# Split f32r products in place of fp32 ones for the first weight of a fused attention and expert kernel

## The chip, the cores and the metric

The kernel runs on one core of a Trainium2 chip, in one launch. The metric is the device time of one execution in microseconds (us). The engines are TensorE (PE, with its weight loads shown apart as PEld), VectorE (DVE), ScalarE (ACT), GpSimd (POOL) and SyncE (SP), which here issues most of the DMAs. Each engine works its own list of instructions in order, and waits on semaphores for the others.

## The reference

Attention over a small set of packed queries, then two feed-forward blocks:

```python
p_packed = softmax(scale * p @ k.T) @ v           # 4 batches, 8 heads, 32 rows of 64
out      = softmax(scale * q @ p_packed.T) @ p_packed
x = out.transpose(0, 2, 1, 3).reshape(2304, 512)  # 4 batches of 576 tokens, 8 heads * 64
h = x @ w_in                                      # 512 -> 2048
x = (max(h, 0) + log1p(exp(-abs(h)))) @ w_out     # softplus, 2048 -> 512
out = (sigmoid(x @ w_gate) * (x @ w_val)) @ w_out2
```

The weights of the two blocks arrive as 64-bit floats; the kernel reads them as pairs of 32-bit words and builds 32-bit floats from them.

## The kernel before

**Stages.** The first stage is attention, worked in eight units of half a batch (`attn_unit`). The second is the softplus block, which overlaps the end of the first. Its hidden width of 2048 is cut into eight chunks `c` of 256 columns. The third is the gated block. The change touches the second stage, and one small operation in the first.

**How x @ w_in is worked.** x of a batch is the second softmax (A2, kept as an f32r pair `A2h`, `A2l`) times the packed rows pp. So the kernel forms pp @ w_in first, for each chunk, and multiplies A2 by that. pp lies in `bdT`, block by block. Chunks 0 and 1 are formed batch by batch (`prep_wp_one`), chunk 2 for two batches at once (`prep_wp_two`), and chunks 3 to 7 for all four (`prep_wp_four`, since `FOUR = 3`). For the last, POOL copies each unit's pp into `ppq` (L472), in an order in which one matmul of 64 rows serves four batches: 128 columns of the array are four batches of 32 rows. Two such matmuls, of the upper and the lower 64 partitions, go to two PSUM banks. They are plain fp32 (L645). ACT copies each bank into a `cv` tile (L652), sixteen DMAs on SP sort its parts by batch into two `xs` tiles (L656), and POOL splits those into f32r pairs `wph` and `wpl` (`split_wp`, `hi_of` and `split_lo`, helper lines L104 and L101).

**The split.** An f32r matmul takes operands cut to fewer bits. To keep the accuracy, an operand is written as hi + lo, and a product as three f32r matmuls: hi*hi, hi*lo, lo*hi (`mm3`, L113 to L115). All large products of the kernel are made so.

**The loop around it.** For a batch b, a chunk c and a half s of its tokens, `emit_h` issues twelve f32r matmuls of 288 columns into a two-bank PSUM tile, ACT forms softplus (L697), ACT and POOL split it into `ghl` (L108, L101), and two turns later `emit_out1` multiplies it by `w_out`: four banks of six matmuls (L725, L726, L728), each added by DVE into `xa` (L733). `ghl` must be complete for the last two of the six.

**What sets the order.** The weights are prepared by generators in a queue `jobs`: `tick()` runs the next step of the first one, and is called four times in each `emit_out1`. `finish(name)` runs all steps that a job still lacks, at the place where its result is used. So a job with more steps ends later in the program, or is forced at `finish`. `prep_win` (conversion of w_in, DVE L180, L185, L189) and `prep_wo` (conversion and split of w_out) of a chunk are queued after the `wp` job of the chunk before. A conversion asks for the next raw weight when it ends, and there are two raw buffers (`NRAW = 2`). The instructions are then ordered on each engine by the framework's scheduler, so that the order on an engine is not that of the program text.

**Buffers.** The `cv` tiles are five, the one-bank PSUM tiles four, the `w_in` tiles two, the two-bank PSUM tiles two.

Of the kernel before, what the change touches and what calls it, by code (L numbers as in the profile page):

```python
# [9 lines left out]
F32 = mybir.dt.float32  # L10
F32R = mybir.dt.float32r
# [3 lines left out]
ALU = mybir.AluOpType  # L15
# [6 lines left out]
def attn_moe_moe_kernel(  # L22
# [21 lines left out]
    nc = tc.nc  # L44
    B, H, S, D = q.shape
    NK = p.shape[2]
# [3 lines left out]
    P = 128  # L50
    NC = 6
    CT = S // NC
    HS = S // 2
# [46 lines left out]
    def split_lo(eng, lo, x, hi):  # L100
        eng.tensor_tensor(lo, x, hi.bitcast(F32), op=ALU.subtract)  # L101

    def pool_hi(hi, x):
        nc.gpsimd.tensor_scalar(hi, x, 1.0, 0.0, op0=ALU.mult, op1=ALU.add)  # L104

    def hi_of(on_act, hi, x):
        if on_act:
            nc.scalar.activation(hi, x, AF.Copy)  # L108
        else:
            pool_hi(hi, x)  # L110
# [54 lines left out]
    def convert(key, dst):  # L165

        t = raws.pop(key)
        hw, lw = t[:, :, 1], t[:, :, 0]  # L170
        if len(dst.shape) == 3:
            hw = hw.rearrange("p (k n) -> p k n", k=KD)
            lw = lw.rearrange("p (k n) -> p k n", k=KD)
        to = x = dst.bitcast(I32)
        if cps[0] and dst.space != PSUM:
            x = bank1()
            if len(dst.shape) == 3:
                x = x.rearrange("p (k n) -> p k n", k=KD)
            x = x.bitcast(I32)
        nc.vector.tensor_scalar(  # L180
            x, hw, 3, 0x3FFFFFF8, op0=ALU.logical_shift_left, op1=ALU.bitwise_and
        )
        if not cps[0]:
            yield
        nc.vector.scalar_tensor_tensor(  # L185
            x, hw, -0x40000000, x, op0=ALU.bitwise_and, op1=ALU.bitwise_or
        )
        yield
        nc.vector.scalar_tensor_tensor(  # L189
            to, lw, 29, x, op0=ALU.logical_shift_right, op1=ALU.bitwise_or  # L190
        )
        load_next()
# [84 lines left out]

    bdT = ph1.tile([P, 2 * B + 2, P], F32, name="bdT")

    ppq = ph1.tile([P, 2 * KD // 2, B, NK], F32, name="ppq")  # L280

    pT = [att.tile([P, 4 * P], F32, name=f"pT{i}") for i in range(2)]
    for t in pT:
# [61 lines left out]
    def heads(tile_, start, step):  # L345

        return tile_[:, start : start + 2 * step].rearrange("p (j x) -> p j x", x=step)[
            :, :, :NK
        ]
# [33 lines left out]
    def attn_unit(u):  # L383
# [81 lines left out]
        for e in range(2):  # L465
            r = slice(64 * e, 64 * e + 64)
            to = bdT[r].rearrange("p j n -> p (j n)")
            copy(
                BDA, heads(to, 512 * half + 256 * g + 64 * odd + 32 * e, 64 if odd else 192),
                heads(pp[r], 32 * e, 64),  # L470
            )
            nc.gpsimd.tensor_scalar(  # L472
                ppq[r, 2 * g : 2 * g + 2, b],
                heads(to, 512 * half + 256 * g + 64 * odd + 32 * e, 64 if odd else 192),
                1.0, 0.0, op0=ALU.mult, op1=ALU.add,
            )
        yield
        a2s = []
        for hf in range(2):
# [84 lines left out]
        return xa[:, i : i + KD * HS].rearrange("p (m t) -> p m t", m=KD)  # L564

    def prep_win(c):
        wt = ph1.tile([P, KD, CF], F32, tag="w_in", bufs=2, name="w_in")
        for f in range(2):
            yield from convert(("in", c, f), wt[:, :, f * P : (f + 1) * P])
            yield  # L570
        w_in_f[c] = wt
# [60 lines left out]

    xs = {}

    def prep_wp_four(c):

        wt = w_in_f[c]
        for half in range(2):
            xs[half, c] = ph1.tile([P, 2, 2, CF], F32, tag="xs", bufs=3, name="xs")
        for j in range(2):  # L640
            ps = [bank1().rearrange("p (t n) -> p t n", t=2) for _ in range(2)]
            for t in range(2):
                for e in range(2):
                    r = slice(64 * e, 64 * e + 64)
                    nc.tensor.matmul(  # L645
                        ps[e][:, t, :], ppq[r, 2 * t + j].rearrange("p b n -> p (b n)"),
                        wt[r, 2 * t + j, :], start=True, stop=True,
                    )
            yield
            for e in range(2):  # L650
                x = new_cv().rearrange("p (t n) -> p t n", t=2)
                nc.scalar.activation(x, ps[e], AF.Copy)  # L652
                for b in range(B):
                    half, odd = divmod(b, 2)
                    o = 64 * (odd ^ j) + 32 * e
                    nc.sync.dma_start(xs[half, c][o : o + 32, odd], x[32 * b : 32 * b + 32])  # L656
                yield

    def split_wp(half, c):
        for odd in range(2):  # L660
            hi, lo = wp_tiles()
            x = xs[half, c][:, odd]
            hi_of(WPH, hi, x)
            split_lo(nc.gpsimd, lo, x, hi)
            Wp[2 * half + odd, c] = (hi, lo)
            yield

    def prep_wp_half(half, c):
        if c < FOUR:
            yield from prep_wp_two(half, c)  # L670
            return
        if half == 0:
            yield from prep_wp_four(c)
        yield from split_wp(half, c)

# [157 lines left out]
    def new_cv():  # L833
        return cv.tile([P, DM], F32, tag="cv", name="cv")
# [323 lines left out]
```

## Time and profile before

| | us |
|---|---|
| median of 3 runs | 861.76 (861.45 to 863.3) |
| the profiled execution | 862.72 |
| span of its instructions | 860.6 |
| PE busy | 839.2 (98%) |
| DVE busy | 588.4 (68%) |
| POOL busy | 479.8 (56%) |
| ACT busy | 326.5 (38%) |

Some 2 us of the execution lie outside the span. Busy times overlap each other. A matmul's duration in the trace runs from its start until its last result is out, so neighbours overlap: the pace of a stream of matmuls is the distance between starts, not the duration. An fp32 matmul stands in the trace as two records.

### The profile page before, as it was taken

How to read it: one execution, taken by the hardware profiler on the slowest of the kernel's cores; microseconds unless marked ns; L12 is line 12 of the kernel's file. 1: busy time of each engine (PE TensorE's matmuls, PEld its weight loads, DVE VectorE, ACT ScalarE, POOL GpSimd, SP SyncE). 2: the span in 40 equal slices, each digit the busy share in tenths (PEclk: the TensorE clock that was granted, in tenths of full speed). 3: DMA queues.
4: the chain of work that ended last, by engine and by line, in shares of the span. 5: the costliest groups of instructions: out<-in, count | busy, mean ns of one | idle time of the engine just before them, and what ended most of it. 6: DMA issues, size and time to landing. Idle time of an engine off the chain costs nothing. (4 is left out here: it accounts for less than half of the span.)

```text
span 860.6 us, 15689 instructions
## 1 busy us (share of the span) xinstructions
PE 839.2 (98%) x6112; PEld 783.0 (91%) x6112; DVE 588.4 (68%) x1004; ACT 326.5 (38%) x606; POOL 479.8 (56%) x469
## 2 busy tenths in 40 slices
PE   7899999999999999999989999999999999999997
PEld 5788989899989999999989999999989999999996
DVE  2776556946656375458788688897896656767665
ACT  4467575563333333434323422232352432322210
POOL 4564333245647364594579786886983734536400
PEclk9999999999999999999999999999999999999999
DMA  9984320203363233500155464644525412213003
GB/s 236 222 206 103 84 59 26 74 25 108 114 178 101 73 98 82 167 5 1 37 171 156 151 177 149 191 129 136 159 55 154 122 41 84 68 43 111 13 1 110
DMA packets 61864, 90.79 MB, mean 105 GB/s; under 512 B 7648, under 2 KB 40544, under 8 KB 61792
## 3 DMA queue, kind: packets, MB, share of 16 engines
q1 hardware_dynamic: 60784, 88.56, 36.9%
q10 hardware_dynamic: 1008, 1.25, 0.4%
q8 instruction: 48, 0.79, 0.4%
q14 instruction: 24, 0.20, 0.1%
HBM read 65.67 MB, written 18.87 MB: 98 GB/s over the span
## 5 line engine op out<-in xcount | busy, mean ns | idle before, releaser
L113 PE MATMUL bank<-aop,BH 128*128 128x288 f32 x672 | 199.1, 296 | 5.0 <-DVE work L1026 2.1
L115 PE MATMUL bank<-aop,BL 128*128 128x288 f32 x672 | 198.6, 296 | 0.0
L114 PE MATMUL bank<-aop,BH 128*128 128x288 f32 x672 | 197.8, 294 | 0.2 <-DVE aop L101 0.2
L733 DVE TENSOR_TENSOR xa<-xa,ps 128x288 f32<-128x288 f32 x224 | 99.5, 450 | 100.3 <-PE ps L728 100.1
L101 POOL TENSOR_TENSOR ghl<-g,ghl 128x576 fp32r<-128x576 f32 x64 | 93.5, 1463 | 132.1 <-ACT ghl L108 113.1
L725 PE MATMUL ps<-ghl,woh 128*128 128x288 f32 x512 | 146.4, 301 | 2.0 <-ACT cv L652 1.3
L726 PE MATMUL ps<-ghl,wol 128*128 128x288 f32 x512 | 143.6, 295 | 0.0
L113 PEld LDWEIGHTS bank<-aop,BH 128*128 128x128 f32 x672 | 126.2, 188 | 10.8 <-issue 2.5
L114 PEld LDWEIGHTS bank<-aop,BH 128*128 128x128 f32 x672 | 126.4, 188 | 4.2 <-DVE aop L101 0.4
L115 PEld LDWEIGHTS bank<-aop,BL 128*128 128x128 f32 x672 | 126.6, 188 | 0.0
L101 POOL TENSOR_TENSOR BL<-cv,BH 128x512 fp32r<-128x512 f32 (+1 forms) x96 | 117.2, 1235 | 3.4 <-ACT BH L108 2.4
L728 PE MATMUL ps<-ghl,woh 128*128 128x288 f32 x512 | 109.1, 294 | 0.1
L725 PEld LDWEIGHTS ps<-ghl,woh 128*128 128x128 f32 x512 | 96.2, 188 | 5.6 <-ACT cv L652 1.6
L726 PEld LDWEIGHTS ps<-ghl,wol 128*128 128x128 f32 x512 | 96.3, 188 | 0.2
L1026 DVE TENSOR_TENSOR work<-work,bank 128x576 f32<-128x576 f32 (+1 forms) x100 | 70.8, 725 | 31.5 <-PE bank L115 31.3
L1074 PE MATMUL ps<-ol,gv 128*128 128x512 f32 x216 | 84.9, 393 | 0.0
L1073 PE MATMUL ps<-oh,gv 128*128 128x512 f32 x216 | 84.3, 390 | 0.5 <-ACT gv L1039 0.4
L1075 PE MATMUL ps<-oh,gv 128*128 128x512 f32 x216 | 84.7, 393 | 0.0
L728 PEld LDWEIGHTS ps<-ghl,woh 128*128 128x128 f32 x512 | 82.2, 188 | 0.5 <-POOL ghl L101 0.5
L1081 DVE TENSOR_TENSOR xa<-xa,ps 128x512 f32<-128x512 f32 x90 | 61.5, 683 | 28.5 <-PE ps L1075 28.0
L104 POOL TENSOR_SCALAR BH<-cv 128x512 fp32r<-128x512 f32 (+1 forms) x48 | 30.0, 634 | 88.1 <-PE bank L114 87.8
L113 PE MATMUL ps<-A2h,wph 128*128 128x288 f32 x256 | 77.3, 302 | 0.4 <-ACT wph L595 0.4
(137 smaller groups left out, 1613.7 us busy)
## 6 DMA issues: line engine op xcount, KB each, us to landing
cv<-B SPq DMA_DIRECT2D x52, 256.0 KB, 2.7
B<-cv SPq DMA_DIRECT2D x48, 256.0 KB, 4.1
raw_in<-in_moe_w_in_dram SPq DMA_DIRECT2D x16, 512.0 KB, 3.7
raw_out<-in_moe_w_out_dram SPq DMA_DIRECT2D x16, 512.0 KB, 3.5
raw_g<-in_moe_w_gate_dram SPq DMA_DIRECT2D x12, 512.0 KB, 4.1
raw_v<-in_moe_w_val_dram SPq DMA_DIRECT2D x12, 512.0 KB, 4.4
raw_o<-in_moe_w_out_dram SPq DMA_DIRECT2D x12, 512.0 KB, 4.1
xs<-cv SPq DMA_DIRECT2D x80, 64.0 KB, 2.0
```

Source lines behind the costliest of these rows:

```text
L101: eng.tensor_tensor(lo, x, hi.bitcast(F32), op=ALU.subtract)
L113: nc.tensor.matmul(ps, wh, xh, start=first, stop=False)
L114: nc.tensor.matmul(ps, wh, xl, start=False, stop=False)
L115: nc.tensor.matmul(ps, wl, xh, start=False, stop=last)
L725: nc.tensor.matmul(out_, wh[:, ms], gh[:, f], start=f == 0, stop=False)
L726: nc.tensor.matmul(out_, wl[:, ms], gh[:, f], start=False, stop=False)
L728: nc.tensor.matmul(out_, wo_hl[c, f][0][:, ms], gl[:, f], start=False, stop=f == 1)
L733: nc.vector.tensor_tensor(dst, dst, out_, op=ALU.add)
L1026: nc.vector.tensor_tensor(to, x, y, op=ALU.add)
L1073: nc.tensor.matmul(bank, gh[:, ts_], oh, start=f == 0, stop=False)
L1074: nc.tensor.matmul(bank, gh[:, ts_], ol, start=False, stop=False)
L1075: nc.tensor.matmul(bank, gl[:, ts_], oh, start=False, stop=f == 1)
```

## The change

pp @ w_in of chunks 3 to 7 becomes three f32r products of split operands in place of one fp32 product.

- `ppq` becomes a pair of f32r tiles. It is no longer filled unit by unit in `attn_unit`. A generator `prep_ppq` of eight steps fills it at the start of chunk 3's `wp` job: 16 roundings (`pool_hi`) and 16 subtractions, all on POOL, each of 64 partitions by 64 elements.
- `prep_win` of chunks 3 to 7 converts into a `cv` tile; ACT rounds it into `hi` (`hi_of`, `WHA = 1`) and POOL subtracts (`split_lo`). The pair takes both `w_in` buffers, so that one chunk is held at a time, not two.
- `prep_wp_four` issues 12 f32r matmuls of 64 rows by 256 columns for each `j`, in place of 4 fp32 ones: 120 in all in place of 40.
- An `xs` tile is cut into two halves; four of them are held, and for odd chunks the second pair of batches uses the tiles `t1`.

```diff
@@ -277,7 +277,7 @@
 
     bdT = ph1.tile([P, 2 * B + 2, P], F32, name="bdT")
 
-    ppq = ph1.tile([P, 2 * KD // 2, B, NK], F32, name="ppq")
+    ppq = [ph1.tile([P, KD, B, NK], F32R, name=f"ppq{y}") for y in "hl"]
 
     pT = [att.tile([P, 4 * P], F32, name=f"pT{i}") for i in range(2)]
     for t in pT:
@@ -469,11 +469,6 @@
                 BDA, heads(to, 512 * half + 256 * g + 64 * odd + 32 * e, 64 if odd else 192),
                 heads(pp[r], 32 * e, 64),
             )
-            nc.gpsimd.tensor_scalar(
-                ppq[r, 2 * g : 2 * g + 2, b],
-                heads(to, 512 * half + 256 * g + 64 * odd + 32 * e, 64 if odd else 192),
-                1.0, 0.0, op0=ALU.mult, op1=ALU.add,
-            )
         yield
         a2s = []
         for hf in range(2):
@@ -564,6 +559,17 @@
         return xa[:, i : i + KD * HS].rearrange("p (m t) -> p m t", m=KD)
 
     def prep_win(c):
+        if c >= FOUR:
+            hl = [ph1.tile([P, KD, CF], F32R, tag="w_in", bufs=2, name="w_in") for _ in "hl"]
+            for f in range(2):
+                x = new_cv().rearrange("p (k n) -> p k n", k=KD)
+                yield from convert(("in", c, f), x)
+                hi, lo = (y[:, :, f * P : (f + 1) * P] for y in hl)
+                hi_of(WHA, hi, x)
+                split_lo(nc.gpsimd, lo, x, hi)
+                yield
+            w_in_f[c] = hl
+            return
         wt = ph1.tile([P, KD, CF], F32, tag="w_in", bufs=2, name="w_in")
         for f in range(2):
             yield from convert(("in", c, f), wt[:, :, f * P : (f + 1) * P])
@@ -632,20 +638,46 @@
 
     xs = {}
 
+    def prep_ppq():
+
+        for b in range(B):
+            half, odd = divmod(b, 2)
+            for e in range(2):
+                r = slice(64 * e, 64 * e + 64)
+                for g in range(2):
+                    src = heads(
+                        bdT[r].rearrange("p j n -> p (j n)"),
+                        512 * half + 256 * g + 64 * odd + 32 * e, 64 if odd else 192,
+                    )
+                    hi, lo = (y[r, 2 * g : 2 * g + 2, b] for y in ppq)
+                    pool_hi(hi, src)
+                    split_lo(nc.gpsimd, lo, src, hi)
+                yield
+
+    def xs_tile(half, c):
+        if half and c % 2:
+            t = ph1.tile([P, 2, HS], F32, tag="t1", bufs=2, name="t1")
+            t = t.rearrange("p f t -> p (f t)")[:, : 2 * CF]
+        else:
+            t = ph1.tile([P, 2 * CF], F32, tag="xs", bufs=4, name="xs")
+        return t.rearrange("p (t n) -> p t n", t=2)
+
     def prep_wp_four(c):
 
         wt = w_in_f[c]
         for half in range(2):
-            xs[half, c] = ph1.tile([P, 2, 2, CF], F32, tag="xs", bufs=3, name="xs")
+            xs[half, c] = [xs_tile(half, c) for _ in range(2)]
         for j in range(2):
             ps = [bank1().rearrange("p (t n) -> p t n", t=2) for _ in range(2)]
             for t in range(2):
-                for e in range(2):
-                    r = slice(64 * e, 64 * e + 64)
-                    nc.tensor.matmul(
-                        ps[e][:, t, :], ppq[r, 2 * t + j].rearrange("p b n -> p (b n)"),
-                        wt[r, 2 * t + j, :], start=True, stop=True,
-                    )
+                J = 2 * t + j
+                for n, (x, y) in enumerate(((0, 0), (0, 1), (1, 0))):
+                    for e in range(2):
+                        r = slice(64 * e, 64 * e + 64)
+                        nc.tensor.matmul(
+                            ps[e][:, t, :], ppq[x][r, J].rearrange("p b n -> p (b n)"),
+                            wt[y][r, J, :], start=n == 0, stop=n == 2,
+                        )
             yield
             for e in range(2):
                 x = new_cv().rearrange("p (t n) -> p t n", t=2)
@@ -653,13 +685,13 @@
                 for b in range(B):
                     half, odd = divmod(b, 2)
                     o = 64 * (odd ^ j) + 32 * e
-                    nc.sync.dma_start(xs[half, c][o : o + 32, odd], x[32 * b : 32 * b + 32])
+                    nc.sync.dma_start(xs[half, c][odd][o : o + 32], x[32 * b : 32 * b + 32])
                 yield
 
     def split_wp(half, c):
         for odd in range(2):
             hi, lo = wp_tiles()
-            x = xs[half, c][:, odd]
+            x = xs[half, c][odd]
             hi_of(WPH, hi, x)
             split_lo(nc.gpsimd, lo, x, hi)
             Wp[2 * half + odd, c] = (hi, lo)
@@ -670,6 +702,8 @@
             yield from prep_wp_two(half, c)
             return
         if half == 0:
+            if c == FOUR:
+                yield from prep_ppq()
             yield from prep_wp_four(c)
         yield from split_wp(half, c)
```

**POOL, where chunk 3's products are split.** POOL's list before; `ghl` is a softplus result of chunk 2, `wph` and `wpl` are chunk 3's pair, one for each batch, `xs` their source:

```order
L101 TENSOR_TENSOR ghl_2812<-g32_2774,ghl_2812 128x576
L101 TENSOR_TENSOR ghl_2884<-g32_2848,ghl_2884 128x576
L104 TENSOR_SCALAR wph_2872<-xs_2753 128x512
L101 TENSOR_TENSOR wpl_2873<-xs_2753,wph_2872 128x512
L104 TENSOR_SCALAR wph_2887<-xs_2753 128x512
L101 TENSOR_TENSOR wpl_2888<-xs_2753,wph_2887 128x512
L104 TENSOR_SCALAR wph_2922<-xs_2754 128x512
L104 TENSOR_SCALAR wph_2934<-xs_2754 128x512
L101 TENSOR_TENSOR wpl_2923<-xs_2754,wph_2922 128x512
L101 TENSOR_TENSOR wpl_2935<-xs_2754,wph_2934 128x512
L101 TENSOR_TENSOR ghl_2946<-g32_2912,ghl_2946 128x576
```

The same place on POOL now, after the same two `ghl` of chunk 2; `w_in_2981` is the lo half of chunk 4's w_in, `wol_3069` and `wol_3111` are chunk 4's w_out:

```order
L101 TENSOR_TENSOR w_in_2981<-cv_2982,w_in_2980 128x4x128
L101 TENSOR_TENSOR w_in_2981<-cv_3010,w_in_2980 128x4x128
L101 TENSOR_TENSOR wol_3069<-cv_3050,woh_3068 128x512
L101 TENSOR_TENSOR wol_3111<-cv_3080,woh_3110 128x512
L104 TENSOR_SCALAR wph_2933<-xs_2877 128x512
L101 TENSOR_TENSOR wpl_2934<-xs_2877,wph_2933 128x512
L104 TENSOR_SCALAR wph_2937<-xs_2878 128x512
L101 TENSOR_TENSOR wpl_2938<-xs_2878,wph_2937 128x512
L104 TENSOR_SCALAR wph_2941<-t1_2879 128x512
L104 TENSOR_SCALAR wph_2968<-t1_2880 128x512
L101 TENSOR_TENSOR wpl_2942<-t1_2879,wph_2941 128x512
L101 TENSOR_TENSOR wpl_2969<-t1_2880,wph_2968 128x512
```

Four operations of chunk 4's weights now stand ahead of chunk 3's first `wph`; before they stood after all of chunk 3's. The row that follows these is `ghl_2994`, the first softplus result of chunk 3.

**SP, the DMAs that sort chunk 3's products.** Before, where a row with x2 is two DMAs; `raw_out_2709` and `raw_out_2739` are the two halves of chunk 4's w_out:

```order
L656 DMA xs_2753<-cv_2798 32x512 x2
L656 DMA xs_2754<-cv_2798 32x512 x2
L656 DMA xs_2753<-cv_2829 32x512 x2
L656 DMA xs_2754<-cv_2829 32x512 x2
L656 DMA xs_2753<-cv_2858 32x512 x2
L656 DMA xs_2754<-cv_2858 32x512 x2
L155 DMA raw_out_2709<-in_moe_w_out_dram 128x1024
L155 DMA raw_out_2739<-in_moe_w_out_dram 128x1024
```

And now, from the fifth of the sixteen on; `raw_out_2701` and `raw_out_2731` are the same two halves:

```order
L688 DMA xs_2877<-cv_2901 32x512
L688 DMA xs_2878<-cv_2901 32x512
L688 DMA t1_2879<-cv_2901 32x512
L155 DMA raw_out_2701<-in_moe_w_out_dram 128x1024
L688 DMA t1_2880<-cv_2901 32x512
L155 DMA raw_out_2731<-in_moe_w_out_dram 128x1024
L688 DMA xs_2877<-cv_2921 32x512
L688 DMA xs_2878<-cv_2921 32x512
L688 DMA t1_2879<-cv_2921 32x512
L688 DMA t1_2880<-cv_2921 32x512
L688 DMA xs_2877<-cv_2927 32x512
L688 DMA xs_2878<-cv_2927 32x512
```

The two loads of w_out have moved from behind the sixteen DMAs to between them.

**PE, from chunk 3's products to their first use.** Counted in PE's list: before, chunk 3's eight fp32 matmuls stand in two groups of four, 22 matmuls apart, and 66 others stand between the second group and the first that reads `wph_2872`. Now all 24 f32r matmuls stand together, and 48 others (the eight banks of two `emit_out1` of chunk 2) stand between them and the first that reads `wph_2933`, `ps2_2945`. For chunk 4 the count is 99 before and 108 now, for chunk 5 108 and 108, for chunk 6 90 and 90, for chunk 7 104 and 104. Behind `ps2_2945` PE has:

```order
L762 MATMUL ps1_3072<-ghl_2862,woh_2396 128x288
L762 MATMUL ps1_3072<-ghl_2862,woh_2448 128x288
L113 MATMUL ps2_2945<-A2h0_114,wph_2933 128x288
L114 MATMUL ps2_2945<-A2l0_118,wph_2933 128x288
L115 MATMUL ps2_2945<-A2h0_114,wpl_2934 128x288
```

Before, the matmuls on `wph_2872` and `wph_2887` are mixed with those of chunk 2's last `emit_out1`; now 36 matmuls of `emit_h` for chunk 3 (24 of the first batch, 12 of the second) come in a row, and then the first bank on `ghl_2994`.

## Rows read from the trace of the kernel before

**Rows 1.** The page, busy time: us, share of the span, instructions.

```profile
PE 839.2 (98%) x6112; PEld 783.0 (91%) x6112; DVE 588.4 (68%) x1004; ACT 326.5 (38%) x606; POOL 479.8 (56%) x469
```

**Rows 2.** Busy time by stretch: us, PE, PEld, DVE, ACT, POOL, granted clock, DMA.

```profile
200.00:240.00 40.00, 40.00 (x301) 38.97 (x300) 28.66 (x56) 15.38 (x25) 23.96 (x20) 1.00 0.47 133
240.00:280.00 40.00, 38.68 (x289) 37.38 (x289) 24.33 (x49) 13.33 (x22) 22.43 (x21) 1.00 0.46 137
```

**Rows 3.** Timeline, PE, around a group of fp32 products: start, duration, instruction.

```profile
213.95 0.42 PE L728 MATMUL ps<-ghl,woh 128*128 128x288 f32 x2
214.30 1.13 PE L645 MATMUL ps<-w_in,ppq 64*128 64x256 f32 x8
215.36 0.40 PE L725 MATMUL ps<-ghl,woh 128*128 128x288 f32 x1
215.60 0.30 PE L726 MATMUL ps<-ghl,wol 128*128 128x288 f32 x1
215.73 0.30 PE L725 MATMUL ps<-ghl,woh 128*128 128x288 f32 x1
```

**Rows 4.** Timeline, PE, full-height fp32 matmuls and f32r ones of 512 columns.

```profile
192.13 1.02 PE L611 MATMUL ps<-w_in,bdT 128*128 128x256 f32 x4
...
848.13 0.39 PE L1074 MATMUL ps<-ol,gv 128*128 128x512 f32 x1
848.36 0.39 PE L1075 MATMUL ps<-oh,gv 128*128 128x512 f32 x1
```

**Rows 5.** Timeline, SP, DMA issues of chunks 3 and 4.

```profile
211.84 11.01 SPq L656 DMA_DIRECT2D xs<-cv  x16
225.65 4.94 SPq L155 DMA_DIRECT2D raw_out<-in_moe_w_out_dram  x2
...
254.05 5.61 SPq L656 DMA_DIRECT2D xs<-cv  x9
```

**Rows 6.** DMA issues: count, KB each, median us from issue to landing.

```profile
raw_out<-in_moe_w_out_dram SPq DMA_DIRECT2D x16, 512.0 KB, 3.5
...
xs<-cv SPq DMA_DIRECT2D x80, 64.0 KB, 2.0
```

**Rows 7.** Timeline, DVE, a conversion of w_out between additions of output banks.

```profile
230.50 0.69 DVE L180 TENSOR_SCALAR ps<-raw_out 128x512 int32<-128x512 int32 x1
231.22 0.70 DVE L185 SCALAR_TENSOR_TENSOR ps<-raw_out,ps 128x512 int32<-128x512 int32 x1
231.83 0.45 DVE L733 TENSOR_TENSOR xa<-xa,ps 128x288 f32<-128x288 f32 x1
232.19 0.68 DVE L189 SCALAR_TENSOR_TENSOR cv<-raw_out,ps 128x512 int32<-128x512 int32 x1
```

**Rows 8.** Timeline, ACT, copies of products and a rounding of w_out.

```profile
215.46 1.09 ACT L652 ACTIVATE cv<-ps 128x512 f32<-128x512 f32 x2 [1.89 <-PE ps L645]
...
233.66 0.62 ACT L108 ACTIVATE woh<-cv 128x512 fp32r<-128x512 f32 x1
```

**Rows 9.** Timeline, POOL, splits of chunk 3 and what follows.

```profile
222.49 0.62 POOL L104 TENSOR_SCALAR wph<-xs 128x512 fp32r<-128x512 f32 x1 [1.49 <-DMA xs<-cv]
223.19 1.29 POOL L101 TENSOR_TENSOR wpl<-xs,wph 128x512 fp32r<-128x512 f32 x1
...
230.09 2.83 POOL L101 TENSOR_TENSOR ghl<-g,ghl 128x576 fp32r<-128x576 f32 x2
```

**Rows 10.** Timeline, PE, the longest wait between 200 and 280 us.

```profile
248.02 0.40 PE L725 MATMUL ps<-ghl,woh 128*128 128x288 f32 x1 [1.32 <-ACT cv L652]
```

**Rows 11.** Timeline, POOL, the first copies into ppq.

```profile
23.16 0.89 POOL L472 TENSOR_SCALAR ppq<-bdT 64x64 f32<-64x64 f32 x2 [5.16 <-ACT bdT L96]
24.16 1.62 POOL L354 TENSOR_SCALAR x<-xa 96x768 f32<-96x768 f32 x2
```

**Rows 12.** Waits of the PE weight loads, 15 to 165 us: total, times, longest.

```profile
PEld ps L365 <- POOL x L354: 3.0, 3, 1.7
```

**Rows 13.** Timeline, PE, bf16 matmuls of 512 columns at the start.

```profile
1.45 5.30 PE L272 MATMUL ps<-hot 128*128 128x512 bf16 x12 [1.45 <-DVE hot L269]
```

## The prediction

> **What bounds the kernel now.** I read the busy times first, then the busy time by stretch, then the timelines of PE, POOL, DVE, ACT and SP around chunk 3's products. PE is busy 839.2 of 860.6 us [rows 1]; from 200 to 240 us it has 40.00 of 40 and 301 matmuls, one each 0.133 us [rows 2]. So there a matmul removed is a gain at its pace, work of other engines costs nothing until PE waits for it, and every such wait is a loss that nothing gives back. POOL is busy 24.0 of those 40 us, ACT 15.4, DVE 28.7.
>
> **The products on PE.** A group of four fp32 products costs this: the last matmul ahead starts at 213.95 + 0.13, so its successor would start at 214.21; the second behind the group starts at 215.60, which puts the first at 215.47. The group cost 1.26 us [rows 3]. Full-height fp32 records of 256 columns start (1.02 - 0.38) / 3 = 0.213 us apart [rows 4]. The group has eight such records of half height: one after another they would need 1.70, and they took 1.26. They run as four pairs, upper and lower half side by side, 0.85, and 0.41 goes into the change from full height to half and back. Ten groups: 12.6 us.
>
> An f32r matmul of 64 rows is nowhere in the trace. Full-height ones take 0.133 for 288 columns [rows 2] and 0.23 for 512 [rows 4]; the line through both gives 0.119 for 256. In pairs, six pairs and the change of height are 6 x 0.119 + 0.41 = 1.12; eight such groups and the double one of chunk 3 (12 x 0.119 + 0.41 = 1.84) make 10.8. Bounds: the lower is half of that pace, since two halves cannot beat twice a pace that I took from full height (8 x 0.77 + 1.12 = 7.3); the upper is no overlap of the halves (8 x 1.84 + 3.27 = 18.0). I take the pairs, as the fp32 rows run: 10.8 - 12.6 = **-1.8 us**, between -5.3 and +5.4.
>
> **What lies beside other work.** ACT gets 10 roundings of 0.6 us [rows 8], POOL 10 subtractions of 1.29 [rows 9]: 6 and 13 us over some 160 us in which they have more than that free. They cost nothing while PE has its operands early; without that cover each POOL one puts off a `ghl` by 1.3. One `w_in` buffer pair in place of two costs nothing, as a chunk's job starts after the last chunk's products anyway. The DMAs stay 80.
>
> In the attention stage POOL gets 16 subtractions of about 0.3 us (a pair of such small operations took 0.89, the copies behind it 0.81 each [rows 11]), some ahead of the copies `x` that feed PE. PE waited for those 3.0 us in three places [rows 12]. Bounds: 0 (POOL idled 5.16 ahead of the first) and 16 x 0.3 = 4.8. I take **+0.3**, near the lower end, since only three places wait.
>
> In chunk 4 PE lost 1.32 us to an ACT copy that lacked a `cv` buffer [rows 10]. POOL's work on the gate weights, which freed it, now stands further ahead of the products. Bounds -1.3 and +1.3; I take **-0.6**.
>
> **Chunk 3: what the new order makes late.** POOL works in order, and now has four operations of chunk 4's weights ahead of `wph_2933`. The last, `wol_3111`, needs the second half of w_out, whose load stands on SP between the sorting DMAs and waits there for a raw buffer. Take t = 0 where PE reaches chunk 3's products.
>
> - PE: products until 1.8, then eight banks of six, 0.80 each: they end at 2.6, 3.4, 4.2 and so on, the last at 8.2. There it wants `wph_2933`.
> - DVE frees the raw buffer with the last step of w_in's second half, which stands behind the addition of the fifth bank. From the second bank's addition (3.7) on, its list alternates additions and steps; by the distances in [rows 7] (0.72 step to step, 0.61 step to addition, 0.36 addition to step) the step ends at 8.4.
> - SP asks for the load at 8.4; it lands 3.5 later [rows 6], at 11.9. In the trace both w_out loads were issued within 4.94 us, behind the sixteen [rows 5].
> - DVE by then does the last steps of the first half and an addition, until 12.3, then three steps: 14.4. ACT rounds, 0.62 [rows 8]: 15.0. POOL subtracts, 1.29: 16.3. Then `wph_2933`, 0.62 [rows 9]: 16.9.
> - So PE waits from 8.2 to 16.9: 8.7 us. After two matmuls it wants `wpl_2934`, done at 16.3 + 0.70 + 1.29 = 18.3: 1.1 more.
> - POOL still has three such pairs ahead of `ghl_2994`: 16.3 + 4 x 1.95 = 24.1, and 1.43 for the `ghl` [rows 9]: 25.6. PE has 34 matmuls of `emit_h` and four of the next bank, until 18.3 + 38 x 0.133 = 23.4: 2.2 more.
>
> Together **+12.0 us**. The additions of banks that PE makes late wait too, but they end the same chain, so PE's last position is unchanged. Bounds: if SP could ask for the second load right behind the first, at 6.8, and it landed as the 64 KB ones do (2.0), all would be 3.1 earlier: 8.9. If every DVE step waited and the loads took a us longer: 14. Without POOL's order the sorting DMAs would be late by themselves: each issue takes 0.62 (5.61 for nine [rows 5]), the last four go out behind the w_out load, and the last part of the first `xs` would land at 8.8 + 4 x 0.62 + 2.0 = 13.3, a wait of 5.7. In the trace before, the same sixteen were spread over 11.01 us, POOL itself waited 1.49 for them [rows 5, 9], and PE did not wait, having 66 matmuls and its second group still to do.
>
> **The sum.** -1.8 - 0.6 + 0.3 + 12.0 = +9.9 on the profiled execution, 862.72 (span 860.6 and 2.1 around it): 872.6. That execution lies 0.96 over the median of the runs, so 871.7 is what the runs should show. Its own range is +6 to +14: 868 to 876.
>
> **Rivals.**
>
> *The queue is clear in time* (faster). If `wol_3111` is done by 8.2 - 0.62 - 1.29 = 6.3, PE finds `wph` and `wpl` as before, and only the -1.8 and -0.6 count: 859.7. For it: POOL has 16 of 40 us free, and PE did not wait here before. Against it: the load cannot be asked for before a raw buffer is free, and 3.5 of flight and 4 of DVE, ACT and POOL follow. It decides at 8.2 us behind the start of the products.
>
> *The halves do not overlap in f32r.* Then the groups cost 18.0 and the total is 7.2 higher, 879. For it: no row shows such a matmul. Against it: the fp32 rows overlap. In the trace each full-height f32r matmul has its own weight load and the pair still passes in 0.133 [rows 2], so loads are hidden behind matmuls of the same rows. The Trainium skill's page TensorE: Matmul & The Clock Gate, section Part 3: Packing small matmuls, says that a weight load overlaps matmuls in flight only where the row groups differ. By that rule, with its 128 / 1.2 = 107 ns for a load, a pair would take an estimated 0.107 + 0.107, and the gain on PE would turn into a loss of about 4 us; the trace's 0.133 speaks against it.
>
> *The clock falls in the pause.* At the start 512 columns take (5.30 - 0.63) / 11 = 0.42 us [rows 13], and 0.23 later [rows 4]: the first is 1.2 GHz. The granted clock is 1.00 in both stretches of [rows 2], where PE never waits over 1.32; 8.7 us without a matmul is not in the trace. If PE came back at 1.2 GHz, the 38 matmuls would take up to 38 x 0.266 = 10.1, ending at 28.4 in place of 25.6: up to +2.8, 874.5; a shorter slow stretch is swallowed by the wait for `ghl_2994`. The same page, section Part 1: The HAM clock gate, says that the clock falls to 1.2 GHz when TensorE has been idle and rises after renewed work; no stretch here shows the fall.
>
> **Chances.** The forecast 0.68, the clock 0.15, no overlap 0.09, a clear queue 0.05, and 0.03 for a wait of some 2 us that just cancels the gain. A measurement of this kernel can tell 0.2% (1.7 us) from no change. So faster 0.05, the same 0.03, slower 0.92. The range takes in the forecast's own and reaches to the clock's and towards the case without overlap: 866 to 878.
>
> **What would show it.** One wait of PE for POOL's `wph`, 7 to 10 us long, at the first `emit_h` of chunk 3 (between 215 and 240 us of the span), a short one for `wpl`, and one of about 2 us for `ghl`; POOL waiting there for ACT's rounding of w_out, ACT for DVE, DVE for the load. The groups of products at 1.1 us in place of 1.26, pairs starting together. Chunks 4 to 7 without new waits. I am wrong if PE has no wait above 3 us in that stretch, or if the groups take 1.8.

## The result and the profile after

| | before | changed kernel |
|---|---|---|
| median of the runs, us | 862.53 (861.45 to 864.92) | 873.48 (871.76 to 877.17) |
| ratio, 95% interval | | 1.0129 (1.0085 to 1.0173) |
| profiled execution (span), us | 862.72 (860.6) | 875.13 (873.3) |

The change makes the kernel 11 us slower: a median of 873.48, where 871.7 was forecast. Medians are over all runs of a kernel; the ratio was not formed from them and is not quite their quotient. The page's busy times, for [rows 1]:

```profile
PE 841.9 (96%) x6152; PEld 787.3 (90%) x6152; DVE 589.7 (68%) x1004; ACT 332.6 (38%) x616; POOL 497.7 (57%) x495
```

PE's busy time hardly moved, its share fell. Busy time by stretch, as in [rows 2], shows where:

```profile
200.00:240.00 40.00, 29.49 (x230) 28.50 (x228) 27.08 (x52) 12.02 (x20) 18.25 (x16) 0.93 0.45 125
240.00:280.00 40.00, 39.16 (x286) 37.98 (x287) 15.95 (x33) 14.53 (x23) 26.83 (x26) 0.95 0.38 103
```

Of 40.00 busy us 29.49 are left, and the granted clock is no longer 1.00. PE's timeline in that stretch, every row that waited:

```profile
228.38 0.40 PE L759 MATMUL ps<-ghl,woh 128*128 128x288 f32 x1 [0.79 <-DVE xa L767]
239.96 0.61 PE L113 MATMUL ps<-A2h,wph 128*128 128x288 f32 x1 [9.72 <-POOL wph L104]
241.31 0.61 PE L115 MATMUL ps<-A2h,wpl 128*128 128x288 f32 x1 [0.50 <-POOL wpl L101]
248.32 0.53 PE L762 MATMUL ps<-ghl,woh 128*128 128x288 f32 x2 [0.34 <-POOL ghl L101]
```

One wait of 9.72 us for `wph`, a short one for `wpl`, and one for `ghl` that is all but closed. The timelines of POOL, DVE and SP tell how it comes about (chunk 3's products start on PE at 220.67):

```profile
227.01 1.28 POOL L101 TENSOR_TENSOR w_in<-cv,w_in 128x512 fp32r<-128x512 f32 x1 [6.41 <-ACT w_in L108]
229.66 1.27 POOL L101 TENSOR_TENSOR w_in<-cv,w_in 128x512 fp32r<-128x512 f32 x1 [1.37 <-ACT w_in L108]
234.35 1.27 POOL L101 TENSOR_TENSOR wol<-cv,woh 128x512 fp32r<-128x512 f32 x1 [3.42 <-ACT woh L108]
238.06 1.26 POOL L101 TENSOR_TENSOR wol<-cv,woh 128x512 fp32r<-128x512 f32 x1 [2.45 <-ACT woh L108]
239.29 0.62 POOL L104 TENSOR_SCALAR wph<-xs 128x512 fp32r<-128x512 f32 x1
...
246.82 4.36 POOL L101 TENSOR_TENSOR ghl<-g,ghl 128x576 fp32r<-128x576 f32 x3
```

```profile
228.24 0.68 DVE L189 SCALAR_TENSOR_TENSOR cv<-raw_in,ps 128x512 int32<-128x512 int32 x1
...
231.17 0.69 DVE L180 TENSOR_SCALAR ps<-raw_out 128x512 int32<-128x512 int32 x1 [1.89 <-DMA raw_out<-in_moe_w_out_dram]
...
235.05 0.70 DVE L180 TENSOR_SCALAR ps<-raw_out 128x512 int32<-128x512 int32 x1 [1.13 <-DMA raw_out<-in_moe_w_out_dram]
```

```profile
228.94 0.35 SPq L155 DMA_DIRECT2D raw_out<-in_moe_w_out_dram  x1
```

Read from the end: `wph` waits in POOL's list behind the second `wol`, that for ACT, ACT for DVE, DVE for the load, and the load was asked for only when DVE had freed a raw buffer (228.92). It landed at 235.0, 6.1 us later. The products themselves, a group of 12 in chunk 4 in place of the eight records of [rows 3]:

```profile
258.29 0.50 PE L677 MATMUL ps<-w_in,ppqh 64*128 64x256 f32 x4
258.63 0.28 PE L677 MATMUL ps<-w_in,ppql 64*128 64x256 f32 x2
258.74 0.40 PE L677 MATMUL ps<-w_in,ppqh 64*128 64x256 f32 x4
258.98 0.28 PE L677 MATMUL ps<-w_in,ppql 64*128 64x256 f32 x2
```

By the distances of starts, the way of [rows 3], a group costs 1.09 to 1.16 us, chunk 3's double one 1.86, all nine 10.74; before, ten groups 12.89.

**The measure used below.** The start of the kernel differs from run to run, so I measure the stretch between two places of PE's list that every kernel has. For the kernel before, the changed kernel and its mended form `x1_nosteps`, PE's timeline:

```profile
157.85 0.40 PE L115 MATMUL ps<-A2h,wpl 128*128 128x288 f32 x1 [0.41 <-DVE wpl L101]
...
422.42 0.40 PE L725 MATMUL ps<-ghl,woh 128*128 128x288 f32 x1 [0.45 <-DVE xa L733]
```

```profile
160.06 0.40 PE L115 MATMUL ps<-A2h,wpl 128*128 128x288 f32 x1 [0.43 <-DVE wpl L101]
...
434.98 0.40 PE L759 MATMUL ps<-ghl,woh 128*128 128x288 f32 x1 [0.44 <-DVE xa L767]
```

```profile
158.62 0.40 PE L115 MATMUL ps<-A2h,wpl 128*128 128x288 f32 x1 [0.41 <-DVE wpl L101]
...
420.55 0.40 PE L758 MATMUL ps<-ghl,woh 128*128 128x288 f32 x1 [0.45 <-DVE xa L766]
```

The stretch is 264.57 before, 274.92 now, 261.93 in `x1_nosteps`.

### The profile page after: what moved, and what is told of

It is laid out like the page before. It is cut to its first block, busy times and chain, and to the rows that moved or that the text cites. A ratio compares the mean times of both kernels' runs of the same rounds, so it can differ in the third digit from the quotient of the medians.

```text
span 873.3 us, 15819 instructions
## 1 busy us (share of the span) xinstructions
PE 841.9 (96%) x6152; PEld 787.3 (90%) x6152; DVE 589.7 (68%) x1004; ACT 332.6 (38%) x616; POOL 497.7 (57%) x495
## 4 chain that ended last, share of the span: by engine, by line
PE 79%; DVE 9%; DMA 5%; ACT 3%; issue 2%; POOL 2%; SPq 0%; DVEq 0%; POOLq 0%; ACTq 0%
PE bank L115 8%; PE bank L113 8%; PE bank L114 8%; PE ps L759 6%; PE ps L762 6%; PE ps L760 6%; PE ps L1107 5%; PE ps L1109 5%; PE ps L1108 5%; PE ps L113 4%; PE ps L115 3%; PE ps L114 3%; PE ps L481 2%; PE ps L365 1%; DMA raw_v<-in_moe_w_val_dram 1%
```

## The experiments

The theory: `prep_ppq` makes chunk 3's `wp` job eight steps longer, the products are forced late, and POOL's list puts chunk 4's weights ahead of `wph`. Its rivals: the split itself costs the time; the fall of the clock does.

Each series had its own runs of the kernel before, with medians of 863.62 (the runs `x1` to `x4`), 863.41 (`x5` to `x8`) and 862.89 (`y`); the ratio is to those.

| kernel | median us | ratio to before, 95% | stretch | start of the stretch |
|---|---|---|---|---|
| x1_nosteps | 859.88 | 0.9975 (0.9952 to 0.9997) | 261.93 | 158.62 |
| y4_nosteps_again | 860.47 | 0.9966 (0.9940 to 0.9992) | 262.15 | 157.57 |
| x2_steps_alone | 874.63 | 1.0133 (1.0115 to 1.0152) | 275.95 | 157.89 |
| x3_hold | 872.43 | 1.0112 (1.0096 to 1.0129) | 273.39 | 158.68 |
| x4_three_raw | 875.53 | 1.0144 (1.0127 to 1.0161) | 270.77 | 163.73 |
| x5_both_j | 861.48 | 0.9967 (0.9945 to 0.9990) | 263.58 | 159.93 |
| x6_hi_only | 860.85 | 0.9970 (0.9942 to 0.9997) | 261.83 | 158.33 |
| x7_changed | 875.65 | 1.0133 (1.0096 to 1.0170) | 274.81 | 161.05 |
| x8_four_steps | 863.03 | 0.9992 (0.9966 to 1.0017) | 265.19 | 161.58 |
| y1_warm | 880.75 | 1.0210 (1.0178 to 1.0241) | 283.50 | 157.46 |
| y2_unit_fill | 864.16 | 1.0007 (0.9977 to 1.0037) | 261.99 | 157.32 |
| y3_late_both | 860.72 | 0.9977 (0.9952 to 1.0002) | 260.96 | 160.52 |

### The steps taken away, and the steps alone

`x1_nosteps` against the changed kernel:

```diff
                     split_lo(nc.gpsimd, lo, src, hi)
-                yield
...
-                yield from prep_ppq()
+                prep_ppq()
```

> The changed kernel, with the 32 POOL operations that fill the pair ppq issued at once at the start of chunk 3's wp job, so that the job has no extra steps. Everything else of the change stays (split w_in, 120 f32r products, the pair in both w_in buffers). In the order the products of chunk 3 stand again in two groups of 12, 71 matmuls ahead of their first use, and no operation of chunk 4's weights stands ahead of the first wph. Theory (the eight extra steps make the job late; the products themselves gain): no wait above 1 us between 215 and 250 us, granted clock full there; the product groups gain 2.15 us and chunk 4's wait of 1.32 us is gone as in the changed kernel's trace, so 2 to 3.5 us under the kernel before, about 860 us. Rival A (the split itself makes it slow: the rounding on ACT, the subtraction on POOL, one chunk of w_in held in place of two): the loss stays, 868 to 874 us. Rival B (the fill of ppq itself delays the attention stage, by the 2.2 us by which the changed kernel's profiled execution was late at 159 us): within 1 us of the kernel before.

`x2_steps_alone` against the kernel before:

```diff
         if half == 0:
+            if c == FOUR:
+                for _ in range(8):
+                    yield
             yield from prep_wp_four(c)
```

> The kernel before, with fp32 products and everything else as it was, and eight empty steps put ahead of the products in chunk 3's wp job. In the order the eight fp32 products of chunk 3 then stand together, 48 matmuls ahead of their first use, and on POOL one wol of chunk 4 stands ahead of the first wph and one between it and the first wpl. Theory (late job): PE stops between 215 and 250 us for 8 to 13 us in all, waiting for wph and wpl, and the time is 9 to 14 us over the kernel before, 871 to 876 us, although no arithmetic has changed. Rival A (the split itself): at most 2 us over the kernel before.

Both came out as the theory has it: by the ratios, the split products without the steps gain 0.25%, 2.2 us, and the steps alone, with fp32 products and no other edit, lose 1.33%, 11.5 us. PE's waits in `x2_steps_alone`:

```profile
234.90 0.61 PE L113 MATMUL ps<-A2h,wph 128*128 128x288 f32 x1 [6.54 <-POOL wph L104]
238.55 0.61 PE L115 MATMUL ps<-A2h,wpl 128*128 128x288 f32 x1 [2.56 <-POOL wpl L101]
```

In `x1_nosteps` no matmul between 205 and 290 us waited 0.2 us or more for another engine. Its row of the busy times by stretch:

```profile
205.00:250.00 45.00, 44.75 (x351) 43.26 (x350) 31.68 (x61) 19.54 (x33) 31.52 (x28) 1.00 0.54 155
```

The rival that the split costs the time has fallen: ACT, POOL and the `w_in` pair do the same work here, and it is hidden. The stretch says where the gain lies: its ten groups cost 11.62 in place of 12.89, 1.27 less, and chunk 4's wait of 1.32 is gone; together that is 2.6 of the 2.64 us. So half of the gain is the products and half is that wait.

### The two links of the chain

`x3_hold` delays chunk 4's weights:

```diff
+                if cc == FOUR + 1:
+                    jobs.append(("hold", (None for _ in range(9))))
                 jobs.append((f"win{cc}", prep_win(cc)))
```

> The changed kernel with all its steps, and nine empty steps put ahead of chunk 4's w_in in the queue. In the order chunk 3's products stay where the change put them (one group of 24, 48 matmuls ahead of their first use), but chunk 4's w_in and w_out leave POOL's list ahead of wph, and their two loads leave SP's list between the sorting DMAs. This parts the two halves of the theory. By the walk on the changed kernel's trace the wait of 9.72 us for wph then shrinks to what the products and the sorting DMAs alone take: PE is out of work at 9.6 us after the products' start, the DMAs of the first xs half are issued by 8.9 to 9.5 us and land 2.0 us later, wph is ready at 12 to 13.5: a wait of 2.5 to 4 us, wpl 0.5 us more, and the wait for ghl grows from 0.3 to about 3, since POOL's eight operations on chunk 3 stay behind one another. In sum 4 to 8 us less than the changed kernel: 866 to 870 us. Rival (POOL's order does not matter, the sorting DMAs or the cover of 48 matmuls set the end): within 2 us of the changed kernel, 871 to 875.

`x4_three_raw`:

```diff
-    NRAW = 2
+    NRAW = 3
```

> The changed kernel with three raw weight buffers in place of two. In the order the products, their cover of 48 matmuls and chunk 4's four operations ahead of wph on POOL all stay; only the loads are issued one buffer earlier, so that chunk 4's w_out is not loaded between DVE's conversions. If the chain through the raw buffer (DVE frees it, the load lands 6.1 us later, DVE converts, ACT rounds, POOL subtracts) is what makes wph late, the wait of 9.72 us shrinks by 2 to 5 us, and the time is 868 to 871.5 us. If the sorting DMAs on SP or POOL's own work set wph's time, the wait stays within 1 us and the time at 872 to 875. A different start of the kernel (loads issued earlier) can move either by about 2 us; the wait itself tells.

By the time both miss. By the wait that they aim at `x3_hold` hits, and `x4_three_raw` goes a little beyond what was expected. PE, POOL and, for the second wait, DVE in `x3_hold`:

```profile
231.45 0.40 PE L113 MATMUL ps<-A2h,wph 128*128 128x288 f32 x1 [3.70 <-POOL wph L104]
...
281.13 0.61 PE L759 MATMUL ps<-ghl,woh 128*128 128x288 f32 x1 [3.06 <-DVE xa L767]
```

```profile
230.78 0.62 POOL L104 TENSOR_SCALAR wph<-xs 128x512 fp32r<-128x512 f32 x1 [11.46 <-DMA xs<-cv]
```

```profile
280.03 0.69 DVE L180 TENSOR_SCALAR ps<-raw_in 128x512 int32<-128x512 int32 x1 [3.06 <-DMA raw_in<-in_moe_w_in_dram]
```

POOL now stands free for 11.46 us and `wph` waits for the sorting DMAs alone: 3.70 and not 9.72. So the place of chunk 4's weights, their operations on POOL and their loads on SP taken together, costs 6.0 of the 9.7, the late products the rest. But what stands behind them in the queue moves back too: DVE converts chunk 4's w_in from 240.72 on, in the changed kernel from 223.29, and the second half of chunk 5's w_in is asked for only at 275.82. DVE waits for that load until 280.03 and PE for DVE, 3.06 us, and a spell of lower clock follows (0.73 from 281 to 287 us). The gain was handed back 50 us later, and 1.5 us of the stretch is left.

In `x4_three_raw` PE's waits were these:

```profile
237.59 0.61 PE L113 MATMUL ps<-A2h,wph 128*128 128x288 f32 x1 [4.06 <-POOL wph L104]
240.72 0.61 PE L115 MATMUL ps<-A2h,wpl 128*128 128x288 f32 x1 [2.04 <-POOL wpl L101]
```

DVE converts chunk 4's w_out there without a wait for a load, and POOL's list came out a little different from what I expected: the second `wol` stands behind the first `wph`. So the wait for `wph` shrinks by 5.7 us, where 2 to 5 was expected, and the one for `wpl` grows by 1.5. The stretch is 4.1 us shorter, as the load was to give, but the start comes 2.7 to 3.7 us later than in the two executions of the changed kernel, and the time shows none of the gain.

### How many steps

`x8_four_steps` yields in `prep_ppq` only from the fifth part on:

```diff
-                yield
+                if 2 * b + e >= 4:
+                    yield
```

> The changed kernel with the same fill of ppq, issued in four steps in place of eight (the first four parts together with the fifth). In the order chunk 3's products are then two groups of 12, 42 matmuls (between the second group and the first use), and of chunk 4's four operations one stands ahead of the first wph on POOL. The theory that the number of steps sets the loss: more than x1_nosteps (none), much less than the changed kernel (11.3 us of waits). Walk from the second group's start: ACT's copies to 2.5 us, the DMAs of the first xs half issued by 4.5 and landed by 6.5, wph at 7.2; PE is there after 1.1 + 42 x 0.133 = 6.7. A wait of 0.5 to 3 us for wph and wpl, another of up to 1.5 for ghl, 861 to 866 us. If instead the order on POOL alone counts, no wait; if the late products alone, as in the changed kernel, 868 or more.

PE waited 1.34 for `wph` and 0.57 for `wpl`, and not for `ghl`: 863.03 us, within the 861 to 866 expected. The stretch is 3.3 us longer than in `x1_nosteps`: the waits, and a spell of 3.4 us at the lower clock behind them, less 0.5 by cheaper groups. Four steps eat what the products gain, eight cost 13 us of stretch.

### What the products cost, and the best version

All three of these start from `x1_nosteps`. `x6_hi_only` leaves out hi*lo and lo*hi of pp @ w_in; `x5_both_j` issues both values of j together, and `y3_late_both` does that for chunks 5 to 7.

```diff
-                for n, (x, y) in enumerate(((0, 0), (0, 1), (1, 0))):
+                for n, (x, y) in enumerate(((0, 0),)):
...
-                            wt[y][r, J, :], start=n == 0, stop=n == 2,
+                            wt[y][r, J, :], start=True, stop=True,
```

> The kernel of x1_nosteps with the products hi*lo and lo*hi of pp @ w_in left out in chunks 3 to 7 (40 matmuls in place of 120); the splits of both operands are still made. It measures the price of the 80 matmuls. If a pair of half-height matmuls passes in 0.12 to 0.13 us and nothing hides it, ten groups shrink from 1.10 to about 0.59 us: 4 to 5.5 us under x1_nosteps, about 855 us. If the two halves of a pair did not run beside each other a group of four would cost 0.9 us or more and the gain would be twice that. If PE's time in these groups is hidden by waits, nothing is gained.

```diff
-        for j in range(2):
-            ps = [bank1().rearrange("p (t n) -> p t n", t=2) for _ in range(2)]
+        four = [[bank1().rearrange("p (t n) -> p t n", t=2) for _ in range(2)] for _ in range(2)]
+        for j, ps in enumerate(four):
...
-            yield
+        yield
+        for j, ps in enumerate(four):
```

> The kernel of x1_nosteps with the products of both values of j issued in one group of 24 for each chunk (five groups of 24 in place of ten of 12; the four one-bank PSUM tiles are then all taken by one group). A group of 12 costs 1.10 us on PE, the group of 24 cost 1.86 in the changed kernel's trace: 2 x 1.10 - 1.86 = 0.34 us for a chunk, 1.7 us for the five. In the order the first use of the products stands 93 to 126 matmuls behind them, in x1_nosteps 71 to 108, so no wait for wph is expected. If the change of matmul height is what a group pays at its ends, 1 to 2 us under x1_nosteps, about 858 us. Rival: the next output banks wait for ACT to empty the four tiles, 0.3 to 1 us for each chunk: no gain, or up to 3 us over x1_nosteps.

```diff
-        for j in range(2):
+        def products(j):
             ps = [bank1().rearrange("p (t n) -> p t n", t=2) for _ in range(2)]
...
+            return ps
+
+        both = [products(j) for j in range(2)] if c >= 5 else None
+        for j in range(2):
+            ps = both[j] if both else products(j)
             yield
```

> The kernel of x1_nosteps with the products of both j in one group of 24 for chunks 5 to 7 alone, where x5_both_j's trace shows 1.85 us for a group and no wait for PSUM, and two groups of 12 for chunks 3 and 4, where it lost 0.8 to 0.9 us inside each group and 2.0 us behind chunk 4's. Expected: three groups of 1.86 in place of six of 1.10 (one of 1.30), 1.0 to 1.2 us under x1_nosteps, about 859 us; the time can hardly tell that, the length of the stretch from 160 to 434 us can. Rival: a wait as in x5_both_j, no gain.

In `x6_hi_only` the ordinary groups cost 0.63 and all of them 7.10 us in place of 11.62, so 80 matmuls are worth 4.5 us, 0.113 for a pair. Yet the stretch is as long as with them, a miss:

```profile
228.73 0.61 PE L115 MATMUL ps<-A2h,wpl 128*128 128x288 f32 x1 [2.25 <-POOL wpl L101]
```

The shorter groups changed the order: one `w_in` operation stands on POOL between `wph` and `wpl`. The wait and a spell of 3.4 us at the lower clock took back 4.0 of the 4.5.

In `x5_both_j` the groups of chunks 5 to 7 cost 1.85 as expected, those of chunks 3 and 4 2.67 and 2.81, and ACT's copies were late for PE's next bank, as the rival had it (the last of them had waited 2.62 us for a DMA of the gate weights, which still read a `cv` tile):

```profile
251.81 0.40 PE L759 MATMUL ps<-ghl,woh 128*128 128x288 f32 x1 [2.00 <-ACT cv L684]
```

`y3_late_both` has the shortest stretch of all, 260.96, 1.0 and 1.2 us under the two runs of `x1_nosteps`, as expected; its time cannot be told from theirs.

> The kernel of x1_nosteps a second time, so that y2_unit_fill and y3_late_both are set beside it on one chip: 859 to 862 us, the stretch from 160 to 434 us as long as in its first run within 0.3 us, while its start may differ by up to 3 us.

It repeats the first run within 0.22 in the stretch. `x1_nosteps` beats both kernels. Against the kernel before it is a small gain: 2.2 and 2.9 us by the ratios of its two series (0.3 to 4.1 and 0.7 to 5.2 by their intervals), 2.6 and 2.4 by the stretch.

### The place of the fill, the clock, and the changed kernel once more

`y2_unit_fill` fills the pair in `attn_unit`, and `prep_ppq` is not called:

```diff
+            src = heads(to, 512 * half + 256 * g + 64 * odd + 32 * e, 64 if odd else 192)
+            phi, plo = (y[r, 2 * g : 2 * g + 2, b] for y in ppq)
+            pool_hi(phi, src)
+            split_lo(nc.gpsimd, plo, src, phi)
```

> The kernel of x1_nosteps with the pair ppq filled unit by unit in the attention stage, where the kernel before fills its one tile, in place of at the start of chunk 3's job. In the order chunk 3's products and their cover of 71 matmuls are as in x1_nosteps. If the place of the fill matters to the attention stage (POOL gets 32 operations there in place of the 16 of the kernel before), the same place of the program that PE reaches at 157.4 us in the kernel before and at 158.2 in x1_nosteps comes 1 us or more later; else it is the same within the spread of the start, 157.4 to 161.2 over the runs so far. Theory: no difference, 859 to 862 us, no wait above 1 us between 205 and 290 us.

The place is reached at 157.32 and the stretch is 261.99, so in this execution the place of the fill cost nothing. Its median, 864.16, lies over the range expected; its runs spread from 859.41 to 869.93. The profiled one (859.46, mean granted clock 0.999) shows no loss; the two longest list a mean clock of 0.989, and what PE waited for in them stays open.

> The changed kernel itself, for its distance from the others on one chip. All theories: 871 to 876 us, waits of 10 to 12 us in all between 215 and 250 us, and its granted clock at half speed for some 10 us from within the pause on.

It did so: 9.12 us for `wph`, and its stretch is within 0.11 of the first.

`y1_warm` puts 31 matmuls into the pause, by turns of 128 and 64 rows:

```diff
+                if (b, c, s) == (0, 3, 1):
+                    warm = bank1()
+                    for n in range(31):
+                        r = slice(0, 64 if n % 2 else P)
+                        nc.tensor.matmul(
+                            warm[:, :HS], wo_hl[2, 0][0][r, :P], A2h[0][r, 0, :HS],
+                            start=n == 0, stop=n == 31 - 1,
+                        )
```

> The changed kernel with 31 further matmuls of 288 columns, by turns of 128 and of 64 rows, into a PSUM tile that nobody reads; in the order all 31 stand behind the eight banks of chunk 2 and ahead of the first matmul on chunk 3's wph, so in the pause of 9.72 us. By the cost of a change of height in the traces they take some 6.6 us, so that PE stands still for 2 to 3 us and not for 9.7. In the order one of the two wol operations of chunk 4 also moves behind the first wph. It asks what the lower clock cost. If the granted clock then stays at full speed and PE's 2.0 us lost to the lower clock (3.9 us of work at half speed behind the pause) are a cost of their own, the time is 2 us or more under the changed kernel's. If that loss lies in the shadow of POOL's list (the ghl that PE needs next comes late anyway), PE waits for ghl by 2 to 3 us in place of 0.3, and the stretch from 160 to 434 us is as long as the changed kernel's within 1 us. I hold the second for likelier.

It failed as a test. The 31 first waited 2.52 us for a PSUM tile, the clock fell, and they took 15.57 us in place of 6.6; PE's timeline, and its busy time by stretch:

```profile
230.25 15.57 PE L1016 MATMUL ps<-A2h,woh 128*128 128x288 f32 x31 [2.52 <-DVE xa L767]
245.62 0.44 PE L113 MATMUL ps<-A2h,wph 128*128 128x288 f32 x1
```

```profile
232.00:249.00 17.00, 17.00 (x41) 10.74 (x42) 2.57 (x4) 0.63 (x1) 5.74 (x6) 0.50 0.23 68
249.00:262.00 13.00, 11.47 (x86) 11.23 (x86) 6.25 (x13) 5.92 (x9) 9.38 (x10) 1.00 0.25 64
```

What the clock costs in the changed kernel is read from its own rows below; a kernel with its pause and the full clock was not had.

## Why the prediction was right, and where its sizes were off

**The chain of chunk 3.** Forecast and measured, from the start of the products (t = 0 at 220.67):

| | forecast | measured |
|---|---|---|
| PE wants `wph` | 8.2 | 9.6 |
| DVE frees the raw buffer | 8.4 | 8.25 |
| the second half of w_out lands | 11.9 | 14.4 |
| DVE has converted it | 14.4 | 16.6 |
| `wph` done | 16.9 | 19.2 |
| PE goes on with `ghl` | 25.6 | 27.6 |

The mechanism holds link by link; the experiments parted its two halves. The mis-sized term is the load: 3.5 us from [rows 6], a median over the kernel, and 6.1 here. The two loads stand between the sorting DMAs, which themselves take longer than the 2.0 of [rows 6]; the DMA issues of the changed kernel between 222 and 240 us, with the median from issue to landing in the last column:

```profile
raw_out<-in_moe_w_out_dram SPq DMA_DIRECT2D x2, 512.0 KB, 5.2
xs<-cv SPq DMA_DIRECT2D x8, 64.0 KB, 2.9
```

In `x3_hold`, where they stand apart, the same DMAs, of the sorting from 220 to 240 us and of w_out from 243 to 252, took what the prediction gave them, so it is their meeting that was left out:

```profile
xs<-cv SPq DMA_DIRECT2D x8, 64.0 KB, 2.0
raw_out<-in_moe_w_out_dram SPq DMA_DIRECT2D x2, 512.0 KB, 3.5
```

PE's own work from the products to that `ghl` is 13.6 us in the walk, so the term is 27.6 - 13.6 = +14.0 where +12.0 was forecast. PE stopped 1.4 later than in the walk (0.79 for an addition, and short gaps between the banks), which only shortens the wait, since POOL's list sets the end. The wait of 5.7 that the prediction gave the sorting DMAs without POOL's order was 3.70 in `x3_hold`, where the two loads were gone from between them as well.

**The products.** Forecast -1.8, measured 12.89 - 10.74 = -2.15. The pairs run side by side: a group cost 1.10 where 1.12 was worked out, and two of the groups before were dearer than the 1.26 of [rows 3] (1.37 and 1.44). The rival of no overlap (1.84 a group) is out. The Trainium skill's rule that a weight load overlaps matmuls in flight only where the row groups differ (page TensorE: Matmul & The Clock Gate, section Part 3: Packing small matmuls) would have made these groups dearer than the fp32 ones; the 1.10 disagrees.

**Chunk 4's wait** of [rows 10]: forecast -0.6, measured -1.32, it is gone. In the stretch +14.0 - 2.15 - 1.32 = +10.5, and 274.92 - 264.57 = +10.35 was measured. That the total came so near +9.9 is luck in part: the chain was forecast 2.0 too short, the two gains 1.1 too small, and the two errors go against each other.

**The attention stage.** Forecast +0.3. The changed kernel reaches the place at 160.06 and 161.05, the kernel before at 157.85; but `x1_nosteps`, one kernel, had 158.62 and 157.57, and `y2_unit_fill` 157.32, so a cost of the fill was not shown and the 2.2 us of the first trace are not explained by it.

**The clock rival** occurred, and in the first trace of the changed kernel it did not decide. The busy time by stretch:

```profile
230.00:240.00 10.00, 0.28 (x3) 0.04 (x2) 5.48 (x9) 1.26 (x2) 4.05 (x5) 0.71 0.73 199
240.00:245.00 5.00, 4.50 (x19) 4.15 (x20) 0.00 (x0) 0.79 (x2) 4.92 (x6) 0.56 0.15 53
```

The clock fell to 1.2 GHz inside the pause, and 4.4 us after PE's return it was back. PE worked some 4 us at half speed and lost 2. But it still had to wait 0.34 for `ghl`, whose time POOL set without a gap from 239.29 on; at full clock it would have come 2 us earlier to the same `ghl`. The prediction had that: a short slow stretch is swallowed by the wait for `ghl`. It was a near thing: in `x7_changed` the lower clock lasted until 247.0, 6.6 us after PE's return, and PE reached `ghl` 0.6 us after POOL had made it, without a wait:

```profile
247.28 1.42 POOL L101 TENSOR_TENSOR ghl<-g,ghl 128x576 fp32r<-128x576 f32 x1
249.28 0.42 PE L762 MATMUL ps<-ghl,woh 128*128 128x288 f32 x2
```

There the clock, and not POOL, set the end of the chain, by about half a us; the load of 5.5 us in place of 6.1 made up for it, and the stretch came out the same.

Where no such wait follows the lower clock counts: `x8_four_steps`' stretch is 3.3 over `x1_nosteps`, its waits are 1.9, and (1 - 0.66) x 5 = 1.7 us went in the spell behind them:

```profile
232.00:237.00 5.00, 4.83 (x25) 4.83 (x26) 2.77 (x4) 1.62 (x3) 4.23 (x5) 0.66 0.65 212
```

The Trainium skill's page TensorE: Matmul & The Clock Gate, section Part 1: The HAM clock gate, says that an idle TensorE falls to the lower clock and that renewed work raises it; the changed kernel's rows agree, while in `y1_warm` PE worked 17 us at 0.50 before the clock rose.

**The rival of a clear queue** is what `x1_nosteps` made true by other means; its 859.7 stands against 859.88 measured. The nearness is luck in part, as the kernel before was at 863.62 in that series and not at 861.76; by the ratio the gain is 2.2 us where the forecast of that rival comes to 2.1.

## What to carry to other kernels

A few cheap operations cost nothing by their work and much by their place: every step that a generator yields moves what stands behind it in the queue, and a result forced at its use loses its cover. Compare the order before and after, count the work between a product and its first use, and look what an in-order engine now has ahead of it. When a link of a chain is taken away, judge by its wait and by a stretch between two fixed places; the time of the whole can hide a gain that is handed back elsewhere.

## What the runs showed of the hardware

- In `y1_warm` the granted clock stayed at 0.50 through 17.00 us in which PE's rows show no idle time: 41 matmuls, by turns of 128 and 64 rows, then full ones. The 31 by turns took 0.50 us each on average.
- Pauses of 2.25 us (`x6_hi_only`) and 1.9 in two pieces (`x8_four_steps`) were followed by 3.4 us at the lower clock. A pause of 2.00 in `x5_both_j` was not: the granted clock is 1.00 from 250 to 262 us there. The kernel before has a wait of 1.32 and no fall. So the length of the pause alone does not tell whether the clock falls.
- Two loads of 512 KB took 5.2 us (median) between sorting DMAs of 64 KB and 3.5 apart from them, the sorting DMAs 2.9 and 2.0 (changed kernel and `x3_hold`).
- The same place of PE's list was reached between 157.32 and 161.58 us in kernels with two raw buffers, and 1 us apart in two runs of one kernel. A difference of 1 us in the time is not seen here without the trace.
